# Between two expert layers: block-wise second products, a sum moved to VectorE, token list before bookkeeping, three transpose banks

## The chip, the cores and the metric

The kernel runs on one core of a Trainium2 chip. The metric is device microseconds (us) of one execution, the median of several; lower is better. Before the change the median of three runs is 818.81 us (817.68 to 820.68). Times inside a trace are counted from the first instruction of the execution. TensorE is PE in the rows, VectorE is DVE, ScalarE is ACT, GpSimd is POOL, SyncE is SP.

## The reference

The work is an attention layer, a first expert layer in which each token picks its best expert, and a second expert layer in which experts pick tokens greedily until each has 384. All is float32.

```python
attn_out = _attn_ref(**attn_kwargs)                       # 4 x 8 heads x 768 x 64
x = attn_out.transpose(0, 2, 1, 3).reshape(3072, 512)

# first expert layer: out = x + gate * (relu(x w1[e]) w2[e]) for tokens with x w_skip > 0
for e in range(8):
    mask = e_idx == e
    h = np.maximum(xc[mask] @ w1[e], 0.0)                 # 512 -> 1024
    y[mask] = gate_w[mask, None] * (h @ w2[e])            # 1024 -> 512
out[do_compute] = xc + y

# second expert layer: (token, expert) pairs in falling order of logit, 384 tokens for each expert
logits = x @ w_gate
for idx in np.argsort(-logits.flatten()):
    tok, e = idx // E, idx % E
    if assigned[tok] >= 0 or counts[e] >= cap: continue
    assigned[tok] = e; counts[e] += 1
for e in range(8):
    h = np.maximum(x[assigned == e] @ w1_2[e], 0.0)
    out[assigned == e] = h @ w2_2[e]
```

## The kernel before

**Units.** Each expert layer is a row of units, one for each expert. A unit gathers its tokens' rows from DRAM (tiles `xg`), turns them 128 tokens at a time with TensorE transposes into a PSUM bank, and splits them into a rounded part `xh` (ScalarE) and a rest `xl` (VectorE). Weights are loaded in chunks of 512 KB (`wr`) and split in the same way into `wh` (ScalarE) and `wl` (GpSimd, or VectorE where `helped` says so). A product is then three matmuls (`P3`: high by high, high by low, low by high). The first products (`mm1`, PSUM `ph`) make eight 128-row pieces `h` of the 1024 hidden values; the second products (`mm2`, PSUM banks `py0` to `py2`) sum over the eight pieces into one bank of 512 values for each block of tokens. In the first layer a unit has 208 slots (`ROWS` is 128 and 80: token blocks 0 and 1); in the second it has 384 (three blocks).

**The end of the first layer.** The last two units of the first layer (`units1[NE:]`, numbers 7 and 8) keep all their `h`, so that the second layer's gate values are known early; their second products come after, from line 1818 on, piece by piece: for each `f`, three matmuls for block 0 and three for block 1 (`mm2`). `rows2_late` then makes the output rows of a unit: ScalarE scales the bank (`o<-py,gwt`), GpSimd adds the input rows (`o<-o,xg`), and GpSimd scatters them into the DRAM table `x2d`, block 0 first and block 1 after it on the same two queues.

**Routing.** In the same stretch the second layer's choice of tokens runs, one phase for each expert. A phase (`phase`) finds the threshold by seven search steps; in each VectorE compares (`gm<-m`), TensorE counts with 24 small matmuls (`pr<-oh,gm`) and one more (`pr<-fl`), and VectorE takes the next digit. Then it makes the expert's mask `fe`, starts the stream that turns the mask into the token list (`slots`, result `ids`), and goes on with the bookkeeping for the next phase: `go`, `part`, `PEN`, `AC`, `rem`, `ML`, then `best()`. Phase 0's list is the first unit's of the second layer.

**What sets the order.** All engines run their instructions in program order, and the program's order is written by a planner. Matmuls call `hook`, which lets streams (routing, lists, turns) issue their next step when a planned clock says that their inputs are there; `wait_for` issues streams' steps until a condition holds. `Stream.when` gives the planned time of a stream's next step; streams of a lower rank go first.

**The change of layers (lines 1825 to 1875).** After the last second product: `wait_for(lambda: 0 in result)`, that is, until phase 0's list is issued; then `split_next()` (weight chunk 0 of the next unit: `wh` on ScalarE, `wl` on VectorE), `units2[0].load()` (three gathers on GpSimd, which need the list and all scatters into `x2d`), `split_next()` twice (chunk 1 with `wl` on VectorE, chunk 2 with `wl` on GpSimd behind the gathers), `wait_for` the three turns, `split_next()` (chunk 3), and `run_units`. A turn (`x_stream`) issues four transposes into the bank `pt`, `xh` on ScalarE, then `xl` on VectorE, and the next turn writes the same bank. The routing stream steps in these waits too. From there on TensorE alternates `mm1` and `mm2` of eight units to the end; the next unit's gathers are issued as soon as its list is there, its three turns by `hook`, and at the latest `split2` waits for them at the unit's start.

Of the kernel before, what the change touches and what calls it, by code (L numbers as in the profile page):

```python
# [7 lines left out]
F32 = mybir.dt.float32  # L8
# [5 lines left out]
OP = mybir.AluOpType  # L14
# [149 lines left out]
def tile_attn_moe_moe(ctx: ExitStack, tc: tile.TileContext, q, k, v, n_global, n_local,  # L164
                      w_skip, w_gate, w1, w2, w2_gate, w21, w22, out):
    nc = Chip(tc.nc)
# [8 lines left out]
    Dm = H * D  # L175
    E, _, F = w1.shape
    KC = Dm // 128
    FC = F // 128
# [6 lines left out]
    HI = -(-SLOTS // 128)  # L185
    ROWS = [min(128, SLOTS - 128 * i) for i in range(HI)]
# [3 lines left out]
    x2d = tc.dram_tile([N, Dm], F32, name="x2d")  # L190
# [247 lines left out]
    NCH = 8  # L438
# [95 lines left out]
    W_ = Weights()  # L534
# [152 lines left out]
    def scatter(dst, ids, src, others):  # L687
        nc.gpsimd.memset(spacer, 0.0)
        st = nc.gpsimd.indirect_dma_start(out=dst, out_offset=bass.IndirectOffsetOnAxis(ap=ids, axis=0),
                                          in_=src, in_offset=None, bounds_check=N - 1, oob_is_err=False)  # L690
        for o in others:
            tc.declare_no_dep(st.ins, o.ins, reason="rows of other tokens")
        others.append(st)
# [166 lines left out]
    slot_rest = slot_ids(gid, sid, gwt, psl, tmp1)  # L860

    class Unit:
        at, tb, py, defer, xh, x2, turns = None, 0, 0, None, None, None, False
        n = [128] * (CAP // 128)

    def x_load(U_, nb):
# [9 lines left out]
    for e in range(E):  # L876
        U_ = Unit()
# [75 lines left out]
    with tc.For_i(0, n_units, 1):  # L953
        with tc.tile_pool(name="lp", bufs=1) as lp, \
# [8 lines left out]
            for c in range(FC):  # L963
                nc.vector.scalar_tensor_tensor(wf[:, KC + c:KC + c + 1], el, float(F), pcol,
                                               op0=OP.mult, op1=OP.add)
                if c:
                    nc.vector.tensor_scalar(wf[:, KC + c:KC + c + 1], wf[:, KC + c:KC + c + 1], 128.0 * c, None,
                                            op0=OP.add)
# [31 lines left out]
            py = lps.tile([128, Dm], F32, name="py")  # L1000
            for c in range(FC):
                nc.tensor.matmul(py, hT[:, c], w2l[c], start=c == 0, stop=c == FC - 1)
            x2 = lp.tile([128, Dm], F32, name="x2")
# [22 lines left out]
    ff = f1x.enter_context(tc.tile_pool(name="f1", bufs=2))  # L1026
# [4 lines left out]
    fps = ctx.enter_context(tc.tile_pool(name="fps", bufs=1, space=bass.MemoryType.PSUM))  # L1031
    P3 = ((0, 0), (0, 1), (1, 0))
# [5 lines left out]
    def turns():  # L1038

        p = fps.tile([128, KC, 128], F32, name="pt")  # L1040
        last_pt[:] = [p[:, :, :]]
        return p

    def x_turn(U_, tb, bank="pt"):
        if tb == 0 and not U_.xh:
            U_.xh = ff.tile([128, KC, width], F32R, name="xh")
            U_.xl = ff.tile([128, KC, width], F32R, name="xl")
        n = U_.n[tb]
        p = fps.tile([128, KC, 128], F32, name=bank) if bank != "pt" else turns()
        p = p[:, :, :n]  # L1050
        for c in range(KC):
            nc.tensor.transpose(p[:, c], U_.xs[tb][:n, c * 128:(c + 1) * 128], ident[:n, :n])
        U_.xt[tb] = p
        nc.scalar.activation(U_.xh[:, :, tb * 128:tb * 128 + n], p, AF.Copy)

    def x_low(U_, tb):
        sl_ = slice(tb * 128, tb * 128 + U_.n[tb])
        nc.vector.tensor_tensor(U_.xl[:, :, sl_], U_.xt[tb], U_.xh[:, :, sl_].bitcast(F32), op=OP.subtract)
# [42 lines left out]
    def mm2(U_, f, h, nb, low):  # L1101
        if f == 0:
            U_.y = [fps.tile([128, Dm], F32, name=f"py{(tb + U_.py) % 3}") for tb in range(nb)]
        ww = W_.parts[U_.g * NCH + 4 + f // 2]
        o = (f % 2) * Dm
        for tb in range(nb):
            for i, (a, b_) in enumerate(P3):
                hook(h[a], ww[b_])
                n = U_.n[tb]
                nc.tensor.matmul(U_.y[tb][:n], h[a][:, tb * 128:tb * 128 + n], ww[b_][:, o:o + Dm],  # L1110
                                 start=f == 0 and i == 0, stop=f == FC - 1 and i == 2)
            if tb == 0 and low:
                low()
        W_.free = 4 * U_.g + (f + 1) // 2
# [24 lines left out]
    def need(chunk):  # L1139
        while chunk not in W_.parts:  # L1140
            b4 = W_.split
            W_.pump(True)
            assert W_.split > b4
# [4 lines left out]
    class Stream:  # L1148
# [11 lines left out]

        def when(self):
            eng, aps = self.need
            if eng == "pt":
                t = ck.ready("pe", last_pt, aps)
                return max(t, ck.at["dve"] + T_LOW) if lows else t
            t = ck.ready(eng, (), aps)
            return max(t, ck.at["dve"] - T_SP) if eng == "dve" else t

    streams = []

    def order():
        return sorted((s_ for s_ in streams if not s_.busy), key=lambda s_: s_.rank())

    def hook(*aps):

        while streams:
            t = max(ck.at["pe"] + T_EPS, ck.ready("pe", (), aps))
            for s_ in order():
                if s_.when() <= t:
                    s_.step()  # L1180
                    break
            else:
                return
# [13 lines left out]
    def flush():  # L1197
        while lows:
            lows.pop()()

    def x_stream(U_):
        for tb in range(len(U_.xs)):
            yield "pt", [U_.xs[tb]]
            x_turn(U_, tb)
            lows.append(lambda tb=tb: x_low(U_, tb))
            yield "dve", [U_.xh[:, :, tb * 128:tb * 128 + U_.n[tb]]]
            flush()
            U_.tb += 1
# [3 lines left out]
    def start(kind, gen):  # L1212
        s_ = Stream(gen)
        s_.kind = kind
        s_.rank = lambda: RANK[kind] if len(result) <= unit_no[0] + T_L else {"x": 0, "turn": 0.5, "main": 1, "ids": 2, "extra": 4}[kind]
        streams.append(s_)
# [62 lines left out]
    x2_st, l2_st = [], []  # L1279
# [7 lines left out]
            scatter(x2d, U_.sid[:n, tb:tb + 1], x2[:n], x2_st)  # L1287
            U_.x2.append(x2)

    def rows2_late(U_):  # L1290
        for tb, n in enumerate(ROWS):
            x2 = ff.tile([128, Dm], F32, name=f"o{tb}", bufs=1)[:n]
            nc.scalar.activation(x2, U_.y[tb][:n], AF.Copy, scale=U_.gw[:n, tb:tb + 1])
            nc.gpsimd.tensor_tensor(x2, x2, U_.xs[tb][:n, :Dm], op=OP.add)
            scatter(x2d, U_.sid[:n, tb:tb + 1], x2, x2_st)

    def epi1(U_, tasks):
        nb = len(U_.xs)
# [310 lines left out]
    def phase(ph_):  # L1609
# [8 lines left out]
        for it, (s_, n_) in enumerate(() if last else BITS):  # L1618
# [22 lines left out]
            else:  # L1641
# [18 lines left out]
                else:  # L1660
                    for j in range(CG):
                        b_ = sels[:, j].rearrange("p a n -> p (a n)") if wide else identh[:CG * n_, j * n_:(j + 1) * n_]
# [23 lines left out]
            else:  # L1686
                dv.scalar_tensor_tensor(nx[:, 1, :nn], val.to_broadcast([128, nn]), s_, nx[:, 0, :nn],
                                        op0=OP.logical_shift_left, op1=OP.bitwise_xor)
# [43 lines left out]
        dv.scalar_tensor_tensor(g1, sc[:, 1], fx[:, 1:2], gq[:, 1], op0=OP.is_le, op1=OP.mult)  # L1732
        dv.tensor_tensor(fe[:, 4], fe_p, g1, op=OP.add)
        start("ids", slots(ph_, fe, fx))
        yield "dve", ()
        go = rt.tile([128, NT, E], BF, name="go")
        part = rt.tile([128, E], BF, name="part")
        dv.tensor_tensor(go, oh, bc_e(gt[:, 0]), op=OP.mult)
# [56 lines left out]
    bank = fps.tile([128, 512], F32, name="py3")[:, :].bitcast(I32)  # L1795
# [21 lines left out]
    W_.on_pool = range(NCH)  # L1817
    for U_ in units1[NE:]:
        U_.py = 2 * U_.defer
        for f in range(FC):  # L1820
            need(U_.g * NCH + 4 + f // 2)
            mm2(U_, f, [t[:, f] for t in U_.h], HI, None)
            W_.pump()
        rows2_late(U_)
    wait_for(lambda: 0 in result)
    f1x.close()
    ff = ctx.enter_context(tc.tile_pool(name="ff", bufs=2))
# [19 lines left out]
    units2 = []  # L1847
    for p in range(E):
        U_ = Unit()
# [16 lines left out]
    def split_next():  # L1866
        need(W_.order[W_.split])

    split_next()
    ck.late = 0  # L1870
    units2[0].load()
    ck.late = 2.0
    split_next()
# [40 lines left out]
```

## Time and profile before

| | us |
|---|---|
| median of three runs | 818.81 (817.68 to 820.68) |
| the profiled execution | 815.27 |
| its span, first to last instruction | 813.5 |
| around the span | 1.77 |
| TensorE busy, share of the span | 751.8, 92% |
| VectorE, ScalarE, GpSimd busy | 531.4, 403.8, 422.6 |

The rows are read in four kinds of view. The page gives the span and the busy time of each engine. The table by stretches gives, for stretches of 2 us, how long each engine was busy and the granted TensorE clock (1.00 is 2.4 GHz, 0.50 is 1.2 GHz). The timeline gives single instructions: start, duration, engine, output and inputs, and in brackets how long the engine was idle before and what is held to have ended that. The DMA views give packets and bytes of each queue in a stretch (q1 carries what SyncE issues, the weight loads among it; q0 what GpSimd issues, the scatters and gathers), and the time from issue to landing.

### The profile page before, as it was taken

Reading aid. Unit: us, or ns where it says so; the run is one execution under the profiler, and the core shown is the slowest. Engines: PE = TensorE matmul, PEld = TensorE weight load, DVE = VectorE, ACT = ScalarE, POOL = GpSimd, SP = SyncE. Lnnn points to the kernel's source line nnn. Section 1 sums busy time; section 2 is a strip of 40 time slices with the busy share of each in tenths; the row PEclk is TensorE's granted clock in tenths of the full one; section 3 lists DMA queues with packets and bytes.
Section 4 is the critical chain, followed back from the end, with each engine's and each line's share of the span. In section 5 each row is a group of like instructions: output and inputs, shape, how many; then the busy total and the mean of one; then the engine's idle time right before and its main releaser. Section 6 shows DMA issues by size and latency. Waiting matters only on the chain.

```text
span 813.5 us, 16951 instructions
## 1 busy us (share of the span) xinstructions
PE 751.8 (92%) x5807; PEld 631.8 (78%) x5807; DVE 531.4 (65%) x1949; ACT 403.8 (50%) x935; POOL 422.6 (52%) x565
## 2 busy tenths in 40 slices
PE   7999999998979889899889938999999999999994
PEld 5887777777669879899678626888788888899993
DVE  6987979989456766667554565878788777722110
ACT  5887788877556445455552123344343434335301
POOL 4554556845032552555442355576584938588401
PEclk9999999999979989999999965999999999999997
DMA  7686998877537646677460071536263444565000
GB/s 184 169 206 181 232 230 217 230 186 212 156 110 245 221 125 187 212 224 248 157 237 6 18 218 50 179 107 222 94 216 131 156 152 134 181 186 190 33 21 39
DMA packets 143831, 132.20 MB, mean 163 GB/s; under 512 B 65427, under 2 KB 110739, under 8 KB 143744
## 3 DMA queue, kind: packets, MB, share of 16 engines
q1 hardware_dynamic: 135360, 111.19, 46.5%
q0 software_dynamic: 6784, 19.51, 7.1%
q8 instruction: 47, 0.77, 0.4%
q10 hardware_dynamic: 1600, 0.39, 0.2%
q14 instruction: 40, 0.33, 0.1%
HBM read 108.80 MB, written 22.79 MB: 162 GB/s over the span
## 4 chain that ended last, share of the span: by engine, by line
PE 59%; DVE 4%; DMA 3%; ACT 2%; issue 2%; POOL 0%; POOLq 0%; SPq 0%; DVEq 0%; ACTq 0%
PE ph L125 27%; PE py L125 25%; PE pr L125 4%; PE pt L125 3%; DMA xg<-xd,gid 1%; DVE wl L125 1%; DMA wr<-in_moe_w_dram 1%; ACT wh L125 1%; ACT xh L125 1%; DVE py L125 0%; DMA xg<-x2d,ids 0%; DVE h L125 0%; DVE xl L125 0%; POOL out_dram L125 0%; ACT ya L125 0%
## 5 line engine op out<-in xcount | busy, mean ns | idle before, releaser
L125 POOL TENSOR_TENSOR wl<-wr,wh 128x1024 fp32r<-128x1024 f32 (+1 forms) x97 | 205.5, 2138 | 107.7 <-ACT wh L125 101.2
L125 ACT ACTIVATE h<-ph 128x208 fp32r<-128x208 f32 (+2 forms) x132 | 54.8, 417 | 216.4 <-PE ph L125 199.1
L125 PE MATMUL py<-wh,h 128*128 128x512 f32 x448 | 158.1, 405 | 0.0
L125 ACT ACTIVATE wh<-wr 128x1024 fp32r<-128x1024 f32 (+1 forms) x148 | 141.5, 984 | 26.4 <-PE py L125 19.7
L125 DVE SCALAR_TENSOR_TENSOR h<-ph,h 128x208 fp32r<-128x208 f32 (+1 forms) x128 | 58.9, 461 | 102.0 <-ACT h L125 101.9
L125 POOL TENSOR_SCALAR pb<-pb,st 128x232 f32<-128x232 f32 (+1 forms) x192 | 83.4, 455 | 75.1 <-ACT pb L125 26.4
L125 ACT ACTIVATE pb<-sb,st 128x232 f32<-128x232 f32 (+1 forms) x192 | 113.8, 664 | 10.5 <-DVE st L125 9.6
L125 PE MATMUL ph<-xh,wh 128*128 128x208 f32 (+1 forms) x512 | 105.2, 322 | 5.9 <-ACT xh L125 2.4
L125 PE MATMUL ph<-xh,wl 128*128 128x208 f32 (+1 forms) x512 | 103.0, 317 | 0.0
L125 PE MATMUL ph<-xl,wh 128*128 128x208 f32 (+1 forms) x512 | 101.7, 318 | 0.0
L125 PEld LDWEIGHTS py<-wh,h 128*128 128x128 f32 x448 | 82.2, 186 | 14.3
L125 PEld LDWEIGHTS ph<-xh,wh 128*128 128x128 f32 x512 | 82.1, 196 | 13.3 <-ACT xh L125 3.2
L125 PE MATMUL py<-wl,h 128*128 128x512 f32 x224 | 90.8, 405 | 0.0
L125 PEld LDWEIGHTS ph<-xl,wh 128*128 128x128 f32 x512 | 82.4, 197 | 1.6 <-issue 1.3
L125 PEld LDWEIGHTS ph<-xh,wl 128*128 128x128 f32 x512 | 82.0, 196 | 0.5 <-issue 0.2
L125 DVE TENSOR_TENSOR wl<-wr,wh 128x1024 fp32r<-128x1024 f32 x51 | 65.9, 1296 | 18.8 <-ACT wh L125 16.9
L125 DVE CUSTOM_DVE_ANT_0 sb<-pS,bias 128x232 f32<-128x232 f32 (+1 forms) x192 | 61.4, 374 | 9.3 <-PE pS L125 7.9
L125 DVE COPY pts<-pP 116x512 f32<-116x512 f32 (+1 forms) x96 | 60.7, 673 | 8.1 <-PE pP L125 7.6
L125 PE MATMUL py<-h,wh 128*128 128x416 f32 x192 | 61.8, 369 | 3.5 <-DVE h L125 3.5
L125 PE MATMUL pS<-kt,qt 64*128 64x232 f32 (+1 forms) x384 | 51.1, 385 | 1.0 <-ACT pb L125 1.0
L125 PE MATMUL pP<-ident,pb 128*116 128x128 f32 (+1 forms) x384 | 51.4, 277 | 0.0
L125 PE MATMUL py<-h,wl 128*128 128x208 f32 x192 | 50.1, 261 | 0.0
(453 smaller groups left out, 1264.1 us busy)
## 6 DMA issues: line engine op xcount, KB each, us to landing
wr<-in_moe_w_dram SPq DMA_DIRECT2D x136, 512.0 KB
xd<-xs SPq DMA_DIRECT2D x32, 192.0 KB
x2d<-xs SPq DMA_DIRECT2D x32, 192.0 KB
kraw<-in_k_dram SPq DMA_DIRECT2D x30, 192.0 KB
qraw<-in_q_dram SPq DMA_DIRECT2D x30, 192.0 KB
vw<-in_v_dram SPq DMA_DIRECT2D x32, 160.0 KB
vw<-in_v_dram SPq DMA_DIRECT2D x32, 120.0 KB
xT<-in_moe_w_dram SPq DMA_DIRECT2D x1, 1536.0 KB
```

The source lines that it names most:

```text
L125: r = f(*a, **k)
```

## The change

Four edits, all between the last products of the first layer and the first of the second.

1. The last unit's second products run a token block at a time (`mm2_block`): all 24 matmuls of block 0, then all 24 of block 1. Block 0's rows are made and scattered after the first half, by ScalarE and GpSimd as before. The unit before it is as it was.
2. The last unit's block 1 rows are made by one VectorE instruction (`scalar_tensor_tensor`: bank times gate plus input rows) in place of a ScalarE and a GpSimd one; the scatter stays on GpSimd.
3. After phase 0 has started its token list, the routing stream gives "hold" as its next need: while a list stream is there its due time is infinite, so bookkeeping and `best()` are issued after the whole list.
4. The first unit of the second layer turns its three blocks in three PSUM banks, `pt`, `py1` and `py2`, in place of one.

```diff
--- before.py
+++ after.py
@@ -860,7 +860,7 @@
     slot_rest = slot_ids(gid, sid, gwt, psl, tmp1)
 
     class Unit:
-        at, tb, py, defer, xh, x2, turns = None, 0, 0, None, None, None, False
+        at, tb, py, defer, xh, x2, turns, banks = None, 0, 0, None, None, None, False, None
         n = [128] * (CAP // 128)
 
     def x_load(U_, nb):
@@ -1160,6 +1160,8 @@
 
         def when(self):
             eng, aps = self.need
+            if eng == "hold":
+                return float("inf") if [s_ for s_ in streams if s_.kind == "ids"] else ck.at["dve"]
             if eng == "pt":
                 t = ck.ready("pe", last_pt, aps)
                 return max(t, ck.at["dve"] + T_LOW) if lows else t
@@ -1200,8 +1202,9 @@
 
     def x_stream(U_):
         for tb in range(len(U_.xs)):
-            yield "pt", [U_.xs[tb]]
-            x_turn(U_, tb)
+            bank = U_.banks[tb] if U_.banks else "pt"
+            yield "pt" if bank == "pt" else "pe", [U_.xs[tb]]
+            x_turn(U_, tb, bank)
             lows.append(lambda tb=tb: x_low(U_, tb))
             yield "dve", [U_.xh[:, :, tb * 128:tb * 128 + U_.n[tb]]]
             flush()
@@ -1287,12 +1290,31 @@
             scatter(x2d, U_.sid[:n, tb:tb + 1], x2[:n], x2_st)
             U_.x2.append(x2)
 
-    def rows2_late(U_):
-        for tb, n in enumerate(ROWS):
-            x2 = ff.tile([128, Dm], F32, name=f"o{tb}", bufs=1)[:n]
+    def row_late(U_, tb, on_dve=False):
+        n = ROWS[tb]
+        x2 = ff.tile([128, Dm], F32, name=f"o{tb}", bufs=1)[:n]
+        if on_dve:
+            nc.vector.scalar_tensor_tensor(x2, U_.y[tb][:n], U_.gw[:n, tb:tb + 1], U_.xs[tb][:n, :Dm],
+                                           op0=OP.mult, op1=OP.add)
+        else:
             nc.scalar.activation(x2, U_.y[tb][:n], AF.Copy, scale=U_.gw[:n, tb:tb + 1])
             nc.gpsimd.tensor_tensor(x2, x2, U_.xs[tb][:n, :Dm], op=OP.add)
-            scatter(x2d, U_.sid[:n, tb:tb + 1], x2, x2_st)
+        scatter(x2d, U_.sid[:n, tb:tb + 1], x2, x2_st)
+
+    def mm2_block(U_, tb):
+        n = ROWS[tb]
+        y = U_.y[tb] = fps.tile([128, Dm], F32, name=f"py{(tb + U_.py) % 3}")
+        for f in range(FC):
+            need(U_.g * NCH + 4 + f // 2)
+            ww = W_.parts[U_.g * NCH + 4 + f // 2]
+            o = (f % 2) * Dm
+            for i, (a, b_) in enumerate(P3):
+                hook(U_.h[a][:, f], ww[b_])
+                nc.tensor.matmul(y[:n], U_.h[a][:, f, tb * 128:tb * 128 + n], ww[b_][:, o:o + Dm],
+                                 start=f == 0 and i == 0, stop=f == FC - 1 and i == 2)
+            if tb == HI - 1:
+                W_.free = 4 * U_.g + (f + 1) // 2
+            W_.pump()
 
     def epi1(U_, tasks):
         nb = len(U_.xs)
@@ -1732,7 +1754,7 @@
         dv.scalar_tensor_tensor(g1, sc[:, 1], fx[:, 1:2], gq[:, 1], op0=OP.is_le, op1=OP.mult)
         dv.tensor_tensor(fe[:, 4], fe_p, g1, op=OP.add)
         start("ids", slots(ph_, fe, fx))
-        yield "dve", ()
+        yield "hold" if ph_ == 0 else "dve", ()
         go = rt.tile([128, NT, E], BF, name="go")
         part = rt.tile([128, E], BF, name="part")
         dv.tensor_tensor(go, oh, bc_e(gt[:, 0]), op=OP.mult)
@@ -1817,11 +1839,18 @@
     W_.on_pool = range(NCH)
     for U_ in units1[NE:]:
         U_.py = 2 * U_.defer
+        if U_.g == E:
+            U_.y = {}
+            for tb in range(HI):
+                mm2_block(U_, tb)
+                row_late(U_, tb, tb == HI - 1)
+            continue
         for f in range(FC):
             need(U_.g * NCH + 4 + f // 2)
             mm2(U_, f, [t[:, f] for t in U_.h], HI, None)
             W_.pump()
-        rows2_late(U_)
+        for tb in range(HI):
+            row_late(U_, tb)
     wait_for(lambda: 0 in result)
     f1x.close()
     ff = ctx.enter_context(tc.tile_pool(name="ff", bufs=2))
@@ -1868,6 +1897,7 @@
 
     split_next()
     ck.late = 0
+    units2[0].banks = ("pt", "py1", "py2")
     units2[0].load()
     ck.late = 2.0
     split_next()
```

## Rows read from the trace of the kernel before

**Rows 1.** The page, its first line.
```profile
span 813.5 us, 16951 instructions
```

**Rows 2.** Stretches: busy us of PE, PEld, DVE, ACT, POOL, then clock.
```profile
474.00:476.00 2.00, 0.00 (x0) 0.00 (x0) 1.68 (x3) 1.06 (x1) 1.74 (x2) 0.50 0.94 330
492.00:503.00 11.00, 10.68 (x74) 8.86 (x75) 5.89 (x18) 3.60 (x5) 4.81 (x3) 0.50 0.18 48
512.00:797.00 285.00, 285.00 (x1673) 242.12 (x1672) 170.76 (x702) 108.30 (x159) 174.92 (x120) 1.00 0.43 143
```

**Rows 3.** Timeline of all engines: the end of the first layer's last unit.
```profile
469.33 1.37 ACT L125 ACTIVATE o<-py,gwt 128x512 f32<-128x512 f32 x2 [15.90 <-PE py L125]
...
469.54 0.40 PE L125 MATMUL py<-wh,h 128*80 128x512 f32 x1
```

**Rows 4.** Timeline of GpSimd: last scatters into x2d, first and third gather.
```profile
471.64 1.04 POOL L125 DMA_INDIRECT x2d<-o,sid  x1 [0.25 <-POOL spacer L125]
...
474.26 1.74 POOL L125 DMA_INDIRECT x2d<-o,sid  x1 [0.26 <-POOL spacer L125]
480.72 1.00 POOL L125 DMA_INDIRECT xg<-x2d,ids  x1 [4.72 <-DVE fl L125]
...
483.29 0.95 POOL L125 DMA_INDIRECT xg<-x2d,ids  x1 [0.30 <-issue]
```

**Rows 5.** Tile x2d from 440 to 500 us: four scatters and three gathers.
```profile
DMA to landing us min/median/max: 2.4/3.7/6.6
```

**Rows 6.** DMA queues, 471:476 then 476:480 us: packets, MB, share.
```profile
q1 hardware_dynamic: 449, 1.64, 100.3%
...
q1 hardware_dynamic: 520, 1.14, 75.0%
q0 software_dynamic: 144, 0.41, 25.6%
```

**Rows 7.** Tile o, whole span, VectorE's one-instruction rows: ns minimum, median, maximum.
```profile
L125 DVE SCALAR_TENSOR_TENSOR o<-pt,gwt,xg x12: 737/748/753, 274.0 to 400.3; 128x512 f32<-128x512 f32 x6, 80x512 f32<-80x512 f32 x6
```

**Rows 8.** Timeline of VectorE: bookkeeping's first and last, the list, chunk 1.
```profile
469.86 0.35 DVE L125 TENSOR_TENSOR go<-oh,py 128x192 bf16<-128x192 bf16 x1
...
472.93 0.15 DVE L125 TENSOR_TENSOR rem<-rem,pr 128x8 f32<-128x8 f32 x1
...
473.90 0.16 DVE L125 SCALAR_TENSOR_TENSOR ids<-pt,ix 128x3 int32<-128x3 f32 x1
...
475.52 1.23 DVE L125 TENSOR_TENSOR wl<-wr,wh 128x1024 fp32r<-128x1024 f32 x1 [0.32 <-ACT wh L125]
```

**Rows 9.** Timeline: second turn's rest, third turn, second layer's first product.
```profile
489.66 0.68 DVE L125 TENSOR_TENSOR xl<-pt,xh 128x512 fp32r<-128x512 f32 x1
...
490.55 1.09 PE L125 MATMUL pt<-ident,xg 128*128 128x128 f32 x4 [0.50 <-PE pr L125]
...
492.32 1.33 PE L125 MATMUL ph<-xh,wh 128*128 128x384 f32 x3 [0.57 <-ACT xh L125]
```

**Rows 10.** Timeline: counts of phase 1's search steps 1, 3 and 4.
```profile
479.46 0.80 PE L125 MATMUL pr<-oh,gm 128*32 128x8 bf16 x24 [6.70 <-DVE gm L125]
...
489.24 0.80 PE L125 MATMUL pr<-oh,gm 128*32 128x8 bf16 x24 [1.21 <-DVE gm L125]
...
493.58 0.80 PE L125 MATMUL pr<-oh,gm 128*32 128x8 bf16 x24
```

**Rows 11.** Timeline: unit 1's first gather, third xh, first product; unit 2's.
```profile
518.30 0.96 POOL L125 DMA_INDIRECT xg<-x2d,ids  x1 [8.37 <-DVE ids L125]
...
534.84 0.60 ACT L125 ACTIVATE xh<-pt 128x512 fp32r<-128x512 f32 x1 [1.42 <-PE pr L125]
...
538.17 0.68 PE L125 MATMUL ph<-xh,wh 128*128 128x384 f32 x3
...
555.25 0.98 POOL L125 DMA_INDIRECT xg<-x2d,ids  x1 [9.21 <-DVE py L125]
...
568.33 0.60 ACT L125 ACTIVATE xh<-pt 128x512 fp32r<-128x512 f32 x1 [1.55 <-PE pr L125]
```

## What the change should do, worked out before it was run

> **What bounds the kernel now.** I read the table by stretches first. From 512 us to 797 TensorE is busy for the whole of 285.00 us at the full clock [rows 2], so in the second layer the end is set by TensorE's own work: what the change can win is an earlier start of that work, and all that TensorE has to do after that start counts against it. Just before, TensorE does nothing at all from 474 to 476 at the lower clock, 1.2 GHz, and from 492 to 503 it is busy again for 10.68 of 11 us, but still at 0.50 [rows 2]. So the hole between the layers costs twice, as idle time and as a slow start.
>
> The timelines say what fills the hole. The first layer's last product ends at 469.94 (469.54 + 0.40) [rows 3], the second layer's first begins at 492.32 [rows 9]: 22.4 us. The chain through it: rows made on ScalarE and GpSimd, the second scatter issued at 474.26, the first gather at 480.72 [rows 4], three turns, the product. The row of that gather names a VectorE instruction as releaser, but its token list was complete at 474.06 (473.90 + 0.16) [rows 8]. What it really needs is the landing of the scatter: the slowest landing in this stretch is 6.6 us [rows 5], and 474.26 + 6.5 is 480.7. The DMA view says why it is slow: from 471 to 476 the weight loads on q1 hold 100.3% of the engines' time and q0 moves not one packet, although a scatter was issued at 471.64 [rows 4, 6]; then, from 476 to 480, q0 moves 0.41 MB, which is both scatters (208 rows of 2 KB) [rows 6].
>
> **Edits 1 and 2, the rows.** The second products are the same 48 matmuls, only in another order; I take their sum as unchanged. Block 0's rows move to the middle of the unit, where ScalarE sits idle (15.90 us before its rows) [rows 3]; that hides them. Were that cover gone, its scatter would be late again and we would be back at before. For block 1 one VectorE instruction takes 0.75 us (737 to 753 ns, for 80 rows as for 128) [rows 7]. It can start at 470.0, ends at 470.75, and with the 0.25 us that GpSimd needs ahead of a scatter [rows 4] the last scatter is issued at 471.0 and not at 474.26: 3.3 earlier. On VectorE the rest of the list is queued behind it and slips by 0.75, which is hidden as the list has 6.7 us to spare before the gather.
>
> When does it land? Taking what the rows show, q0 gets nothing before 476; then 80 rows, 0.16 MB, at 0.41 MB in 4 us take 1.6 us: 477.6, and 0.3 later the first gather: **477.9, 2.8 earlier**. Ends: with the fastest landing, 2.4 us [rows 5], the scatter would be there at 473.4 and the list would be late next, so a gather at about 474.3 (6.4 earlier); if q0 drains only at 480, as now, nothing is won. I take 2.8, since the same loads run at the same time.
>
> The Trainium skill, page "DMA: Bandwidth & Descriptors", section "Issuing engines are not separate DMA queues", says that transfers run on the same 16 engines and interleave whichever engine issued them; by that rule the scatter would share from 471 on. The 5 us without a packet of q0 speak against it here.
>
> **Edit 3, the hold.** Bookkeeping now lies between the list's steps, from 469.86 to 473.08 [rows 8]. Without it the list is ready some 0.5 to 1 us sooner, worth nothing while the scatter is later. What it costs is the other side: `wait_for` ends as soon as the list is issued, and then both weight chunks' `wl` are issued to VectorE before the routing stream's next step. So bookkeeping runs behind the second `wl`, which ends at 476.75 (475.52 + 1.23) [rows 8]. By itself it is at most 3.2 us and I take 2.8, since it has no more list steps between. Phase 1's first count, at 479.46 now [rows 10], can come at 482.3 at the soonest. Moreover the gathers are planned sooner, so the turns stand ahead of that count in TensorE's queue, and it waits for the third: about 485.
>
> **Edit 4, the banks.** The third gather now is issued at 483.29 [rows 4] and lands 3.7 us later (the median) [rows 5], at 487.0. Its turn begins only at 490.55, after `xl` of the second has left the bank at 490.34 [rows 9]: 3.55 us late. With its own bank a turn waits for its gather alone. `py1` and `py2` have long been read by then. The third gather follows the first by 2.57 us [rows 4]: 480.5, landing at 484.2; from the turn to the first product 1.77 us (492.32 - 490.55) [rows 9] and 0.1 for the count between: the first product at **486.1, 6.2 earlier** (2.8 from the scatter, 3.5 from the banks, less 0.1). Ends: 4.0 if the loads of the next chunks slow the gathers, 9 with the early gather above.
>
> **What is given back.** Two things. First, the search steps that now run free in the hole: steps one to three have their counts between 479.46 and 489.24 [rows 10], before TensorE has any product. In a hole that ends at 486.1 only the first fits. Each count is 0.80 us of TensorE [rows 10], 0.85 with the small product behind it; two of them now fall among products: **1.7** (ends 0.85 and 2.55).
>
> Second, the next list. Routing is a chain of its own, and it isn't made faster: with step one at 485 and steps 4.3 apart (489.24 to 493.58) [rows 10], step three comes at 493.6 and not 489.24. That is 4.4 late, or 2.8 if the counts go ahead of the turns; I take 3.9, so unit 1's first gather comes at 522.2 and not 518.30 [rows 11]. From that gather to the start of the third `xh` it took 16.5 us in unit 1 (534.84) and 13.1 in unit 2 (568.33 - 555.25) [rows 11]. Unit 1's first product, 538.17 now [rows 11], is due at 538.17 - 6.2 + 1.7 = 533.7, with slack of 3 us at most even before. With 13.1, since at a unit's start the program waits for the turns and nothing else, `xh` begins at 535.3 and the product at about 535.9: **2.2 us** of TensorE idle. Ends: none, and 5.6 with 16.5.
>
> **The sum.** 6.2 - 1.7 - 2.2 = 2.3 us. The profiled execution took 815.27 for a span of 813.5 [rows 1], so 1.8 lie around it; that execution is 3.5 below the median. I carry the difference over: 813.0 for such an execution, 818.8 - 2.3 = **816.5** as median. Stated otherwise: the hole shrinks by 6 us, but unit 1 can then start only when routing lets it, and that is 2 us sooner than now.
>
> One cost I leave at zero: the slow start. TensorE stays at 0.50 for 11 us after its first product [rows 2], about 5.5 us lost. It is still idle for over 10 us before, so I expect the same; one search step more or less of that stretch (4.3 us) would be 2.1 us either way, and it goes into the range.
>
> **Rivals.**
> *The next list is in time after all* (turns squeezed in by `hook` before unit 1 starts). For it: unit 2's turns took 3.4 us less than unit 1's. Against it: the 3 us of slack now. It gives 6.2 - 1.7 = 4.5, so 814.3.
> *The scatter shares the DMA engines from 471 on*, a gather at 474.3, a first product three us sooner, one count more in the way, and no stall: 4.5 + 3.1 - 0.85 = 6.8, so 812.0. Against it stand the packets [rows 6]. This is the case in which the page's rule holds.
> *The gap hardly shrinks*, that is, edits 1 and 2 don't do what they say: the scatter still drains at 480 with the weights, the gathers are slowed, and only the banks help, by some 2.7 less 1.7: 1.0, so 817.8.
> *Slower: routing becomes the bound at unit 1.* Place: the turns of unit 1, behind the list of phase 1, which the hold has put back. It decides from the point where unit 1's first gather is issued later than 524.4 (538.17 - 0.6 - 13.1), 6.1 later than now. With one search step more lost (4.3) and turns as slow as unit 1's are now: 518.3 + 3.9 + 4.3 + 16.5 + 0.6 = 543.6, 5.4 later than now: 824.2.
>
> **How the numbers follow.** The forecast has 0.50, the list in time 0.20, the shared engines 0.07, the hardly shrunk gap 0.13, the slower case 0.10. A measurement of this kernel can tell about 0.5%, 4.1 us, from no change. Faster by more than that are the second and third case, 0.27; within it the forecast and the small gap, 0.63; slower 0.10. The range goes from 811.5, which takes in both faster cases, to 822.0, which takes in the forecast with a stall of 5.6 and a slow start that is longer by a step (-2.3 + 3.4 + 2.1 = +3.2), and leaves most of the slower case out.
>
> **What would show it.** Edits 1 and 2: the last scatter issued near 471.0, the first gather near 477.9; a gather near 474 means shared engines, one near 480 none of it. Edit 3: phase 1's first count at 482 to 485. Edit 4: three turns without `xl` between, the third within 0.3 of its landing, the first product near 486. Given back: one count before that product in place of three, and TensorE idle for about 2 us ahead of unit 1's first product, with its gather near 522. Wrong altogether would be a first product after 490, or a unit 1 that starts without idle time on TensorE and over 4 us sooner, or over 2 us later, than 538.17.

## The result, and the profile of the changed kernel

The changed kernel takes 822.59 us (821.51 to 824.33) where the kernel before takes 817.22: a ratio of 1.0062, 95% interval 1.0048 to 1.0077. It is **slower by 5.4 us**, 0.6%, clear of its interval and above the top of my range, and by none of the cases that I had written down. (The figure lies near the 824.2 of my slower case. That is chance: unit 1, which was to be late there, kept a lead of 4.3 us, as the table below shows.) The profiled execution has a span of 822.6 us.

In that execution the last product of layer 1 ends at 473.75 us, 3.8 later than in the profile of before [rows 3]. The edits are not the reason, as in the five later profiles that keep edits 1, 2 and 4 it ends between 468.2 and 472.2. So I count from that product in both. From there to the end it is 343.6 us before and 348.9 after: 5.3 more, the whole difference.

Timelines of PE, DVE and POOL in the hole between the layers (start, duration; in brackets idle time and releaser), which answer [rows 3, 4 and 8 to 10]:

```profile
473.35 0.40 PE L125 MATMUL py<-wh,h 128*80 128x512 f32 x1
...
473.84 0.75 DVE L125 SCALAR_TENSOR_TENSOR o<-py,gwt,xg 80x512 f32<-80x512 f32 x1
...
474.86 1.09 POOL L125 DMA_INDIRECT x2d<-o,sid  x1 [5.92 <-DVE tb_rhs L125]
...
477.07 0.16 DVE L125 SCALAR_TENSOR_TENSOR ids<-pt,ix 128x3 int32<-128x3 f32 x1
...
480.33 0.35 DVE L125 TENSOR_TENSOR go<-oh,py 128x192 bf16<-128x192 bf16 x1
...
482.06 1.00 POOL L125 DMA_INDIRECT xg<-x2d,ids  x1 [6.11 <-DVE py L125]
...
485.58 1.09 PE L125 MATMUL pt<-ident,xg 128*128 128x128 f32 x4 [4.07 <-DMA xg<-x2d,ids]
...
487.13 1.09 PE L125 MATMUL py<-ident,xg 128*128 128x128 f32 x4 [0.46 <-DMA xg<-x2d,ids]
...
488.15 0.81 PE L125 MATMUL pr<-oh,gm 128*32 128x8 bf16 x24
...
489.20 0.16 PE L125 MATMUL pr<-fl,wt 32*128 32x8 bf16 x1 [0.24 <-DVE fl L125]
...
489.51 1.09 PE L125 MATMUL py<-ident,xg 128*128 128x128 f32 x4 [0.16 <-issue]
...
491.00 0.80 PE L125 MATMUL pr<-oh,gm 128*32 128x8 bf16 x24 [0.39 <-DVE gm L125]
...
492.21 0.16 PE L125 MATMUL pr<-fl,wt 32*128 32x8 bf16 x1 [0.41 <-DVE fl L125]
...
492.30 1.33 PE L125 MATMUL ph<-xh,wh 128*128 128x384 f32 x3
```

The edits do what they say. The row by VectorE takes 0.75 us, the last scatter leaves 1.1 after the last product (4.3 before), the first gather 8.3 after it (10.8 before), the bookkeeping (`go`) comes behind the list, and two turns go to banks of their own. The hole is 18.55 us where it was 22.38. ScalarE's first `o<-py` of each unit of layer 2, counted from layer 1's last product, says what became of that:

| unit | 0 | 1 | 2 | 3 | 4 | 5 | 6 |
|---|---|---|---|---|---|---|---|
| before, us | 71.3 | 110.4 | 150.4 | 189.4 | 228.5 | 263.9 | 298.9 |
| changed, us | 67.2 | 106.1 | 145.8 | 185.7 | 224.9 | 269.2 | 304.2 |
| difference | -4.1 | -4.3 | -4.6 | -3.7 | -3.6 | +5.3 | +5.3 |

Some 4 us are won and held for 150 us, and then **8.9 us are lost within unit 5**, 200 us away from the edits. The stretches of the changed kernel show the same (busy us of PE, PEld, DVE, ACT, POOL, then clock; they answer [rows 2]):

```profile
492.30:503.30 11.00, 11.00 (x76) 9.01 (x75) 6.01 (x19) 2.38 (x3) 5.99 (x3) 0.50 0.16 48
512.00:700.00 188.00, 187.69 (x1168) 154.18 (x1167) 147.48 (x638) 73.73 (x107) 122.20 (x81) 1.00 0.46 150
700.00:740.00 40.00, 33.77 (x170) 29.38 (x169) 22.54 (x59) 13.53 (x19) 24.87 (x17) 0.91 0.57 184
```

TensorE stays busy up to 700. Of the 40 us after that 6.2 are idle, and the clock, 1.00 before, is 0.91 over them. What stands there, on POOL, DVE and PE:

```profile
707.73 0.95 POOL L125 DMA_INDIRECT xg<-x2d,ids  x1 [0.30 <-issue]
708.71 2.41 POOL L125 TENSOR_TENSOR wl<-wr,wh 128x1024 fp32r<-128x1024 f32 x1
...
711.31 1.01 POOL L125 DMA_INDIRECT out_dram<-o,ids  x1 [0.18 <-issue]
712.35 4.64 POOL L125 TENSOR_TENSOR wl<-wr,wh 128x1024 fp32r<-128x1024 f32 x2
...
708.53 2.63 DVE L125 CAST tb_rhs<-fe 128x24 bf16<-128x24 f32 x1
...
711.77 5.64 DVE L125 SCALAR_TENSOR_TENSOR mp<-islot,fx,ma 128x384 bf16<-128x384 f32 x1
...
717.47 0.26 PE L125 MATMUL pt<-tb_rhs,mp 128*128 128x27 bf16 x3 [6.23 <-DVE mp L125]
...
720.28 1.05 PE L125 MATMUL pt<-ident,xg 128*128 128x128 f32 x4
```

It is the routing's last token list (`slots`, phase 7). Two VectorE instructions of it last until GpSimd's weight subtractions `wl` beside them are done: `tb_rhs` ends at 711.16 with the subtraction of 708.71 to 711.12, `mp` at 717.41, 0.42 after the pair of 712.35 to 716.99. TensorE has the list's product in its queue and waits 6.23 us for `mp`; unit 6's turns (`pt<-xg`) stand behind. What the two take in all eight lists (tiles `mp` and `tb_rhs`, ns minimum/median/maximum). The kernel before:

```profile
L125 DVE SCALAR_TENSOR_TENSOR mp<-islot,fx,ma x8: 617/618/621, 471.8 to 707.2; 128x384 bf16<-128x384 f32 x8
L125 DVE CAST tb_rhs<-fe x8: 167/168/365, 469.8 to 705.4; 128x24 bf16<-128x24 f32 x8
```

The changed kernel:

```profile
L125 DVE SCALAR_TENSOR_TENSOR mp<-islot,fx,ma x8: 617/620/5641, 475.2 to 711.8; 128x384 bf16<-128x384 f32 x8
L125 DVE CAST tb_rhs<-fe x8: 167/168/2629, 473.6 to 708.5; 128x24 bf16<-128x24 f32 x8
```

**Theory 1:** VectorE was held behind GpSimd, 5.0 us in `mp` and 2.5 in `tb_rhs`, because these two want SBUF at the same time as GpSimd's subtraction. The Trainium skill, page "SBUF — State Buffer", section "Who interferes with whom", names two kinds of VectorE instruction that share a port pair with GpSimd under an exclusive lock: those with two SBUF inputs (`mp` reads `islot` and `ma`), against a GpSimd instruction that reads SBUF, and casts in a two-port mode. The two holds above agree with it, 5.64 and 2.63 us; whether `tb_rhs` runs in such a mode no row here shows. **Rivals:** the place of the list's small products in TensorE's queue (2), or the clock as cause and not consequence (3).

### The profile page after: what moved, and what is told of

Its sections match the earlier page's. It is cut to its first block, busy times and chain, and to the rows that moved or that the text cites. A ratio compares the mean times of both kernels' runs of the same rounds, so it can differ in the third digit from the quotient of the medians.

```text
span 822.6 us, 16951 instructions
## 1 busy us (share of the span) xinstructions
PE 752.2 (91%) x5807; PEld 630.3 (77%) x5807; DVE 543.1 (66%) x1950; ACT 403.1 (49%) x934; POOL 421.2 (51%) x564
## 4 chain that ended last, share of the span: by engine, by line
PE 54%; DVE 7%; issue 4%; DMA 3%; ACT 2%; POOL 1%; another core or an unknown queue 0%; SPq 0%; POOLq 0%; DVEq 0%; ACTq 0%
PE ph L125 24%; PE py L125 23%; PE pr L125 4%; PE pt L125 2%; DMA wr<-in_moe_w_dram 2%; DVE wl L125 2%; DVE py L125 1%; DMA xg<-xd,gid 1%; DVE mp L125 1%; ACT wh L125 1%; DVE h L125 0%; DMA xg<-x2d,ids 0%; DVE tb_rhs L125 0%; ACT xh L125 0%
## 5 line engine op out<-in xcount | busy, mean ns | idle before, releaser
L125 PE MATMUL py<-wh,h 128*128 128x512 f32 (+1 forms) x448 | 158.2, 406 | 0.0
L125 ACT ACTIVATE pb<-sb,st 128x232 f32<-128x232 f32 (+1 forms) x192 | 113.8, 664 | 10.8 <-DVE st L125 9.6
L125 PEld LDWEIGHTS py<-wh,h 128*128 128x128 f32 (+1 forms) x448 | 83.0, 187 | 14.9 <-issue 0.3
L125 PE MATMUL py<-wl,h 128*128 128x512 f32 (+1 forms) x224 | 91.7, 409 | 0.0
L125 DVE TENSOR_TENSOR wl<-wr,wh 128x1024 fp32r<-128x1024 f32 x51 | 68.9, 1356 | 18.1 <-ACT wh L125 16.7
L125 POOL DMA_INDIRECT xg<-x2d,ids x24 | 23.1, 964 | 57.7 <-DVE py L125 47.4
```

The costliest lines, as they stand in the source:

```text
L125: r = f(*a, **k)
```

## Experiments

**The port.** Four kernels keep every instruction of every engine in its place and change only where two things of a list lie. (A PSUM operand that would be priced otherwise by the planner is priced as before, so that the order stays.) The running count, which `tb_rhs` copies, moves to PSUM (`run_p`; the two small instructions that read it follow), and so does the comparison `ma`. `a_free` has both moves on the changed kernel, `b_free` both on the kernel before, `a_fe` that of the count and `a_ma` that of `ma` alone on the changed kernel.

```diff
-        dv.tensor_tensor_scan(fe[:, 5], fe[:, 4], wrow_p[:, :NT], 0.0, op0=OP.add, op1=OP.bypass)
-        dv.tensor_copy(ttb, fe[:, 5, NT - 1:NT])
-        dv.tensor_copy(tb_rhs[:, :NT], fe[:, 5])
+        dv.tensor_tensor_scan(run_p, fe[:, 4], wrow_p[:, :NT], 0.0, op0=OP.add, op1=OP.bypass)
+        dv.tensor_copy(ttb, run_p[:, NT - 1:NT])
+        dv.tensor_copy(tb_rhs[:, :NT], run_p)
...
-        dv.tensor_tensor(fx[:, 4:5], pb[:, 0, 0:1], fe[:, 5, NT - 1:NT], op=OP.add)
+        dv.tensor_tensor(fx[:, 4:5], pb[:, 0, 0:1], ttb, op=OP.add)
...
-        ma = rt.tile([128, CAP], F32, name="ma")
+        ma = pb[:, 1:1 + NH].rearrange("p a n -> p (a n)")
```

> The changed kernel, in which every engine has the same instructions in the same order; only the places of two things in each token list differ: the running count (tb_rhs reads it) and the comparison ma (mp reads it) lie in PSUM instead of SBUF, so that neither VectorE instruction takes a second operand or its only one from SBUF beside GpSimd. Theory 1 (in the last list VectorE was held behind GpSimd's subtractions wl: tb_rhs 2.63 us instead of 0.17, mp 5.64 instead of 0.62, 7.5 us in two instructions, and unit 6's turns stood behind them): mp back to 0.62 and tb_rhs to 0.2 or so, the list ends near 711 instead of 718.7, and the 4 us gained up to unit 4 reach the end: 813 to 814.5 us, ratio to the kernel before 0.995. Theory 2 (what costs is that the list's small products stand ahead of unit 6's turns in TensorE's queue, or the turns' order): the order is the same, so 822 to 823, ratio 1.006. Theory 3 (the granted clock, 0.90 in 700:720, is the cause and not the consequence): about 1.006 too, with the clock still low there.

> The kernel before with the same two things in PSUM, again with every instruction in its old place. Theory 1: in the kernel before no instruction of a list was held by more than 0.2 us (mp 0.62 in all eight lists), so nothing is to be had here: ratio 0.999 to 1.001. If the new places are cheaper by themselves, and not because of GpSimd, this kernel gains as the changed one does: ratio below 0.998, and theory 1 loses its support.

> The changed kernel with the comparison ma alone in PSUM (mp then has one operand in SBUF); the copy into tb_rhs still goes from SBUF to SBUF. Theory 1: mp back to 0.62 (5.0 us less), tb_rhs still held by about one subtraction where it meets one (2.4 to 2.6 us, 8 lists), so 815 to 818, ratio 0.997 to 1.001, between the two others. Theory 2 and 3: 822 to 823.

> The changed kernel with the running count alone in PSUM (tb_rhs no longer copied from SBUF to SBUF), mp with both operands in SBUF as in the changed kernel. tb_rhs then isn't held, and mp comes 2.4 us earlier, at about +236.6, inside the subtraction of +234.9 to +237.3. If an instruction is held until that one subtraction ends: mp about 1.4 us instead of 0.62, ratio 0.996 to 0.998. If, once held, it lets GpSimd's further instructions pass too (in the changed kernel mp came 0.6 ahead of a pair of subtractions and ended 0.4 after the pair): mp 4 to 7 us, ratio 1.001 to 1.006. Theory 2 (not the port): as the changed kernel, 1.006, with mp 5.6.

Measured, as ratios to the kernel before: `a_free` **0.9955** (0.9936 to 0.9974), `b_free` 0.9989 (0.9974 to 1.0004), `a_ma` 0.9975 (0.9958 to 0.9991), `a_fe` 0.9967 (0.9951 to 0.9983). The tiles `mp` and `tb_rhs` on VectorE, of `a_free`:

```profile
L125 DVE SCALAR_TENSOR_TENSOR mp<-islot,fx,pt x8: 602/602/606, 472.7 to 707.5; 128x384 bf16<-128x384 f32 x8
L125 DVE CAST tb_rhs<-py x8: 172/172/173, 470.8 to 705.6; 128x24 bf16<-128x24 f32 x8
```

The tile `tb_rhs` of `a_ma`:

```profile
L125 DVE CAST tb_rhs<-fe x8: 167/168/2680, 472.1 to 706.6; 128x24 bf16<-128x24 f32 x8
```

In `a_free` GpSimd still subtracts from 705.86 to 708.28 and `mp` runs at 707.51, inside that time, for 0.61 us. `mp` and `tb_rhs` are not held, and TensorE is busy for all of 700 to 740. Unit 5's first `o<-py` comes 260.3 us after layer 1's last product, against 269.2 in the changed kernel, and the two ratios (1.0062, and 0.9955 of 814.6) are 8.7 us apart: that is the loss in unit 5. Theories 2 and 3 fall: the queue's order is the same, and the clock stays at 1.00. In the kernel before the same two moves are worth 0.1%, within the interval: what they mend is the meeting, not the instructions. `a_ma` is held in `tb_rhs` alone, as forecast, and in its profile unit 5 is 1.4 us later than in `a_free`; the two ratios can't be told apart.

`a_fe` corrects my picture of what a hold costs. Without the hold of `tb_rhs`, `mp` comes at another moment and is not held at all; `ma`, from SBUF to SBUF, meets the subtraction of 703.94 to 706.35 instead (timeline of `a_fe`):

```profile
705.05 1.53 DVE L125 TENSOR_SCALAR ma<-islot,fx 128x384 f32<-128x384 f32 x1
706.62 0.62 DVE L125 SCALAR_TENSOR_TENSOR mp<-islot,fx,ma 128x384 bf16<-128x384 f32 x1
```

The 2.5 us of the first hold had pushed `mp` in front of a pair of subtractions. One hold brought on the next.

**Which part of the change causes the meeting.** Each part alone, once with the lists in PSUM (`bf_`), where `tb_rhs` and `mp` are not held, and once with the lists in SBUF as they were (`b_`): the second products and last rows (`rows`), the hold of the bookkeeping (`hold`), the three banks (`banks`). The hold is one word:

```diff
-        yield "dve", ()
+        yield "hold" if ph_ == 0 else "dve", ()
```

and the banks are

```diff
+    units2[0].banks = ("pt", "py1", "py2")
```

with what answers to them in `when` and `x_stream`, as in the change.

> The kernel before with the lists in PSUM (as b_free, ratio 0.999), and of the change only the last unit's second products a token block at a time and its last rows by VectorE. My forecast's term for it: the first gather of layer 2 comes 2.8 us earlier after the last product (10.8 us before, 8.3 in the changed kernel). If the turns follow it: hole between the layers 22.4 to about 19.7 us, ratio 0.995 to 0.997. If the turns stay behind the routing's counts and fl in TensorE's and VectorE's queues (second turn idle 0.73 until fl in b_free), the gather's gain reaches the first product only in part: hole 21, ratio 0.998. No instruction of a list held by GpSimd in either.

> The kernel before with the lists in PSUM, and of the change only the three banks for unit 0's turns. My forecast's term for it: first product 3.5 us earlier with the gathers where they are (first turn 14.3 after the last product, third turn 20.6, first product 22.4): hole about 18.9, ratio 0.994 to 0.996. Rival: in TensorE's queue two counts stand between the turns (16 of the second count's 24 pieces ahead of the second turn, a third count ahead of the first product), so that banks free what the counts hold anyway: hole 21 to 22, ratio 0.998 to 1.000.

> The kernel before with the lists in PSUM, and of the change only the token list ahead of the bookkeeping. The gather waits for the last scatter, not for the list (list out 4.0 us after the last product, gather 10.8): no gain in the hole, 22 us, while the first counts come later by up to the bookkeeping's 2 us. Ratio 0.999 to 1.001. If the hold matters by displacing counts into layer 2 (1.7 us in my forecast), ratio up to 1.002; if it matters as the list's lead, below 0.998.

> The kernel before with nothing but the second products a block at a time and the last rows by VectorE, lists in SBUF. In bf_rows (ratio 0.9984) tb_rhs comes at +238.3, third gather ends +238.5, wl follows at +238.6. Theory 1: held as in the changed kernel, ratio 1.006 to 1.010. Rival: 0.997 to 1.000.

> The kernel before with nothing but the three banks, lists in SBUF. In bf_banks (ratio 0.9957) the last list's tb_rhs comes at +231.5 and mp at +233.4, beside unit 6's first and second gather, and the first subtraction only at +234.8. Theory 1: nothing held, tb_rhs 0.17 and mp 0.62 as in the kernel before, ratio 0.995 to 0.998: faster than both kernels with a part of the change alone. Rival (every version with units some 4 us earlier meets the subtractions, since these come earlier with the units): about 1.006.

> The kernel before with nothing but the hold (one word in the routing and what answers it), lists in SBUF as they were. In bf_hold (the same with lists in PSUM, ratio 1.0006) the last list's tb_rhs comes at +239.5 us after layer 1's last product, 0.1 ahead of a subtraction wl at +239.7 that follows unit 6's third gather, as in the changed kernel (+234.8 and +235.0). Theory 1 (VectorE held by GpSimd, set off by where the list falls among GpSimd's instructions): tb_rhs and mp held as in the changed kernel, about 7 us, unit 5 or 6 late by about 8, ratio 1.008 to 1.012. Rival (the collision belongs to the larger change, banks and all): 1.000 to 1.002.

| part alone | hole, us | ratio, lists in PSUM | ratio, lists in SBUF | last row of list 6 after unit 4's first `o<-py`, us (PSUM, SBUF) |
|---|---|---|---|---|
| none | 21.2 | 0.9989 (0.9974 to 1.0004) | 1 | 3.6, 3.3 |
| rows | 20.6 | 0.9984 (0.9964 to 1.0003) | **1.0105** (1.0084 to 1.0127) | 6.4, 6.1 |
| hold | 21.6 | 1.0006 (0.9985 to 1.0028) | **1.0100** (1.0077 to 1.0124) | 6.4, 6.0 |
| banks | 19.6 | 0.9957 (0.9937 to 0.9976) | 0.9963 (0.9948 to 0.9978) | 3.6, 3.3 |
| all three | 18.3 | 0.9955 (0.9936 to 0.9974) | 1.0062 (1.0048 to 1.0077) | 6.3, 6.1 |

(The hole is that of the kernel with lists in PSUM. Before and `b_free` have the same order, and their holes, 22.4 and 21.2, differ by 1.2; the first gather was issued 10.8 and 8.9 us after layer 1's last product. So a difference of holes of that size says nothing by itself.) `tb_rhs` and `mp` of the last list in VectorE's timeline, `b_rows`:

```profile
706.70 2.57 DVE L125 CAST tb_rhs<-fe 128x24 bf16<-128x24 f32 x1
...
709.87 5.64 DVE L125 SCALAR_TENSOR_TENSOR mp<-islot,fx,ma 128x384 bf16<-128x384 f32 x1
```

`b_hold`:

```profile
708.45 2.60 DVE L125 CAST tb_rhs<-fe 128x24 bf16<-128x24 f32 x1
...
711.66 5.64 DVE L125 SCALAR_TENSOR_TENSOR mp<-islot,fx,ma 128x384 bf16<-128x384 f32 x1
```

`b_banks`:

```profile
701.72 0.17 DVE L125 CAST tb_rhs<-fe 128x24 bf16<-128x24 f32 x1
...
703.51 0.62 DVE L125 SCALAR_TENSOR_TENSOR mp<-islot,fx,ma 128x384 bf16<-128x384 f32 x1
```

On what is held, all six came out as theory 1 had them (`b_rows` a little above its span of 1.006 to 1.010). Of the gains, the rows bring less than my first reading had and the banks what it had, with less of the hole. One word in the routing costs 1.0% if the lists lie in SBUF, and nothing that can be told from zero if they lie in PSUM. The last column says why it is no chance: the last row of phase 6's list starts either 3.3 to 3.6 us after unit 4's first `o<-py` or 6.0 us and more, and no profile lies between. The routing's steps are placed among the products in TensorE's program order, and the rows as well as the hold shift them by some 2.7 us. The traces show the place: the last list's product stands behind 892 matmul records of layer 2's units in before, `b_free`, `bf_banks` and `b_banks`, and behind 907 in all the others, wherever the lists lie. In the first kind of order the last list runs beside unit 6's first two gathers, and `tb_rhs` and `mp` take their 0.17 and 0.62 us there; in the second it meets the subtraction behind the third one. The change as a whole has the second kind of order.

The banks are the part that pays: alone, with nothing else changed, they are faster than both kernels.

**The counts ahead of the first product.** `af_nohold` is `a_free` without the hold. `af_hold2` is `a_free` with the routing held until unit 0's blocks are turned:

```diff
-                return float("inf") if [s_ for s_ in streams if s_.kind == "ids"] else ck.at["dve"]
+                return float("inf") if [s_ for s_ in streams if s_.kind in ("ids", "x")] else ck.at["dve"]
```

> The changed kernel with the lists in PSUM, without the hold of the bookkeeping. In TensorE's queue a whole count then stands between the first two turns, and another between the third turn and the first product. If the hold matters as my forecast has it, only by what is displaced: the same as a_free within 1 us (ratio 0.995 to 0.997). If the counts between the turns cost what the two counts cost in af_hold2's trace (1.35 us of hole): 0.997. List 1 comes earlier by what the bookkeeping no longer waits, about 2 us, and no unit waits for it.

> The changed kernel with the lists in PSUM as in a_free, and the routing held back until unit 0's three blocks are turned, not only until list 0 is out. It measures the two counts that stand in TensorE's queue ahead of layer 2's first product. By the trace of the changed kernel (third turn at 489.51 behind a count at 488.15, third xh done 491.24, a second count at 491.00, first product 492.30) the hole between the layers, 18.55 us there, shrinks by 1.0 (the second count alone) to 2.5 (the first one too): 811 to 813.5 us. If the routing behind is what a unit waits for (my forecast took 2.2 us for that at unit 1), the gain is given back at unit 1's turns, and the time is that of a_free or more; by the changed kernel's trace list 1 comes at 519.9 and unit 1's turns at 527.7, so there should be room.

Measured: `af_nohold` 0.9970 (0.9950 to 0.9990), not to be told from `a_free`: the hold brings nothing. List 1, which I expected some 2 us earlier, comes 46.1 us after layer 1's last product in both. `af_hold2` **1.0070** (1.0055 to 1.0085), a miss of mine. Its hole is the shortest of all, 16.9 us, and unit 0 ends 62.8 after layer 1's last product (66.9 in `a_free`). But list 1 comes at 53.3 and not at 46.1, unit 1's third turn starts at 538.26 and its first product at 540.04, and unit 1 ends at 117.8 instead of 105.9. The stretch of it (columns as above):

```profile
535.00:555.00 20.00, 15.88 (x96) 12.38 (x96) 14.81 (x65) 7.63 (x11) 10.83 (x7) 0.83 0.23 66
```

That is the slower case of my prediction, routing as the bound at unit 1, in another kernel: list 1 comes 7 us later and unit 1 ends 12 us later. Of these 12, TensorE is idle for 6.0; 1.8 of that stand behind a copy from SBUF to SBUF that a subtraction held for 2.04 us (`c<-fe`, of which more below). The clock, 0.81 between 538.26 and 560, accounts for at most some 4 more (an estimate: 0.19 of 21.74 us).

## Why the prediction was wrong, point by point

- **The step that failed** is the premise that from 512 us on "the end is set by TensorE's own work", so that layer 2 moves as a block. That the routing goes on beside it, and that its order among GpSimd's and TensorE's instructions changes with every edit ahead of it, I used only as far as unit 1. What set the end in its place was the last token list: beside GpSimd's subtractions `tb_rhs` and `mp` took 7.5 us more than elsewhere, TensorE stood idle for 6.2, and unit 5 ended 8.9 later than unit 4's lead promised. This cost of 8.7 us (by the ratios) has no term in my sum and no rival. Without it my sign was right: 2.3 us forecast, 3.7 (2.1 to 5.2) measured in `a_free`.
- **The rows** (last scatter 1.1 after the last product, gather 2.8 earlier): 1.1 and 2.5. The gather's place varies: 8.9 to 11.1 us after the last product in the six profiles without this edit, 7.8 to 9.5 in the eight with it. The scatter, issued at 474.86, again moved nothing at first; DMA queues of the changed kernel, 476:478 and 478:480:

```profile
q1 hardware_dynamic: 200, 0.75, 102.9%
...
q1 hardware_dynamic: 186, 0.66, 85.8%
q0 software_dynamic: 34, 0.11, 13.6%
```

  The rule of the Trainium skill that the prediction cites (page "DMA: Bandwidth & Descriptors", section "Issuing engines are not separate DMA queues"), that transfers interleave whichever engine issued them, did not show in the 3 us up to 478 either: the gather came 8.3 us after the last product, against 4.4 by that case and 8.0 by mine.
- **The hole**, 6.2 us shorter: it was 3.8. Of the 2.4 that are missing, 0.3 is the gather. Then the third turn came 15.8 after the last product and not 14.3, 1.2 beyond the gather's part: in TensorE's queue a whole count and its small product stand ahead of it (488.15 to 489.36). And from the third turn to the first product it was 2.8 us and not 1.9, as a second count does the same. I had allowed 0.1 for one count. `af_hold2` bears this out: with no count there, it takes 8.1 us from the first gather to the first product, where `a_free` and the changed kernel take 10.2. By itself the banks' part is 1.6 to 2.6 us of hole (19.6 and 19.8 against 21.2 and 22.4), not 3.5; counted from the first gather, which varies, it is 2.2 to 3.0 (9.4 in both against 11.6 and 12.3).
- **Counts displaced among products**, 1.7: one count and not two moved behind the first product. Unit 0 took 48.9 us from its first product to its end before and 48.7 after, but that hides a loss: the clock had a second dip before that it didn't have after. The stretch 503:512, before and then changed:

```profile
503.00:512.00 9.00, 8.70 (x62) 6.24 (x62) 4.93 (x27) 2.55 (x4) 6.93 (x3) 0.78 0.02 5
503.00:512.00 9.00, 8.76 (x88) 6.19 (x87) 4.32 (x21) 2.88 (x4) 6.07 (x3) 0.93 0.01 2
```

  By 0.15 of 9 us the dip is worth about 1.3 (an estimate), and TensorE's idle time in unit 0 was 0.8 before and 0.2 after. So what moved cost some 1.7 us, the size of my term, though it was one count and not two; what makes up the rest I have not traced.
- **List 1 late, 2.2 us idle at unit 1**: it did not happen. I took the steps as 4.3 apart from [rows 10]; the three at 488.15, 491.00 and 493.58 are 2.9 and 2.6 apart, and the first gather of unit 1 came 46.6 after layer 1's last product where my working has 52.3. The mechanism is real, as `af_hold2` shows, but begins later.
- **The slow start** was left at zero: 0.50 for 11 us in both, as I expected. The second dip in before, above, I had not looked at.

Why two holds of 7.5 us cost 8.9: 6.2 of it is TensorE's idle time up to `mp`. After it TensorE works at a clock of 0.53, nearly all of it at 1.2 GHz, until 723 us (stretch of the changed kernel):

```profile
717.47:723.00 5.53, 5.53 (x20) 4.65 (x20) 2.09 (x7) 1.55 (x2) 0.82 (x1) 0.53 0.56 160
```

At full speed these 5.53 us would have been 2.6 fewer (an estimate: 0.47 of 5.53), and 6.2 and 2.6 make 8.8. In `a_free`, where TensorE is not idle there, the clock stays at 1.00.

## What to carry to other kernels

An edit that saves time in one place shifts every stream that runs beside the bound; look through the trace of before for short instructions whose longest is far over their median (`tb_rhs`, 365 against 168 ns, beside a scatter, and `c<-fe`, 317 against 171 ns, beside a subtraction, were there to be seen), and ask what the longest would be beside each long GpSimd instruction. For VectorE instructions on a chain that TensorE waits for, while GpSimd computes, it helped here to have one of two operands in PSUM, and to have the source of a copy there: it cost nothing (`b_free`) and took 1.1% off the changed kernel. And try the parts of a change one at a time: the one that paid was a line and what answers to it, and either of the others alone made the kernel slower.

## What the runs showed of the hardware

- Some VectorE instructions that meet GpSimd's 128x1024 subtraction last until it is done, however small they are: `tb_rhs`, 24 elements to a partition, 2.63 us instead of 0.17, and in `af_hold2` a copy of two elements (`c<-fe`) 2.04. `mp` was not let in between two subtractions in a row, 5.64 us instead of 0.62. Held were casts and a comparison (`ma`) from SBUF to SBUF and `mp` with two operands in SBUF. Not held, in the middle of a subtraction, were a reduction from SBUF to SBUF (`ix<-cx`, 0.23 us in `b_free`, at 698.72) and a one-element instruction with its tensor in SBUF (`tb_rhs<-fx`, 0.16 us in `af_hold2`, at 717.63).
- A recorded start ahead of the subtraction did not help: `tb_rhs` is recorded 0.18 us ahead and `mp` 0.58 ahead, and both were held. The Trainium skill, page "SBUF — State Buffer", section "Who interferes with whom", says that whichever issues first has the pair for its whole instruction. These rows don't decide whether that holds, since GpSimd was not free at either start: the third gather ran from 707.73 to 708.68 and a scatter from 711.31 to 712.32, and each ended 0.03 us before its subtraction began.
- A scatter's issue can hold a cast as well. In the kernel before:

```profile
660.20 1.00 POOL L125 DMA_INDIRECT out_dram<-o,ids  x1 [5.90 <-ACT o L125]
...
660.81 0.36 DVE L125 CAST tb_rhs<-fe 128x24 bf16<-128x24 f32 x1
```

  It lasts until 0.02 to 0.03 us before the scatter ends, and so do the five others in these traces that start 0.60 to 0.62 us into such a scatter (0.36 to 0.38 us each). `c<-fe`, which starts 0.24 to 0.26 into one, takes 0.17 in all 14 profiles. All four held `tb_rhs` (changed kernel, `a_ma`, `b_rows`, `b_hold`) start in the last 0.21 us of unit 6's third gather, so whether the gather or the subtraction began the hold is not separated.
- The issue of a gather did not hold `mp`: in the kernel before it ran its 0.62 us beside the gather of 706.75 to 707.71.

```profile
706.75 0.96 POOL L125 DMA_INDIRECT xg<-x2d,ids  x1 [0.31 <-issue]
...
707.18 0.62 DVE L125 SCALAR_TENSOR_TENSOR mp<-islot,fx,ma 128x384 bf16<-128x384 f32 x1
```

- With one of the two operands in PSUM `mp` took 0.60 us in all eight lists, beside a subtraction too.
